# GpSimd issues the DMAs of its own weight sums, `outer` is laid out in column halves, and the hidden sums are spread one tile a group

## The chip, the cores and the metric

The program runs on one core of a Trainium2 chip. The metric is the device time of one execution in microseconds; the profile comes from one further execution of the same program. An engine's name is followed by its short form in the rows: TensorE (PE, its weight loads PEld), VectorE (DVE), ScalarE (ACT), GpSimd (POOL), SyncE (SP, which here only issues DMAs; SPq in the rows).

## The reference

4608 tokens in 8 batches of 576. First an attention within chunks of 64 tokens (8 heads of 64), then a gated layer without routing, all in float32:

```python
scores = scale * np.matmul(q_c, k_c.transpose(0, 1, 2, 4, 3))   # chunks of 64
attn = np.exp(scores - max); attn = attn / (sum + 1e-09)
x = np.matmul(attn, v_c)                                        # to [4608, 512]
gate = 1.0 / (1.0 + np.exp(-(x @ w_gate)))                      # 512 -> 1536
out = (gate * (x @ w_val)) @ w_out                              # 1536 -> 512
```

## The kernel before

**Precision.** Each float32 operand is split into a high and a low part that TensorE takes at full rate, and each product is three matmuls (high x high, low x high, high x low). The low part is always made by a subtract on VectorE after a copy on ScalarE.

**Blocks.** The tokens are nine blocks of 512. Blocks 0, 1 and 2 go through `hidden` and `down`: for each of 12 tiles `f` of the hidden width, 24 matmuls of 128x512 for gate and value, and 12 into four accumulators `acc` (one per 128 tokens); after `f` = 11 `evacuate` copies these to `ob` or, for the third and fourth of block 2, to `obs`, and stores them.

Blocks 3 to 8 go in three pairs n = 0, 1, 2. A pair uses a seven-product scheme for 2x2 block matrices, so that it has seven products where eight would stand. The *up stage* has 12 groups (6 pairs `p` of hidden tiles, gate and value), each with 7 products of 6 matmuls (`first`, `middle`, `last`); the weights of a group come from HBM as `wr` (`load_group`), half of them the blocks themselves (`given`), half of them sums of blocks (`sums`). The *down stage* has 42 *spots*, one for each of 7 products and 6 tiles `f`, with 6 matmuls each (`down_products`, L620): its weights `wd` come from `outer` (the blocks) and `outer_sums` (`load_down`), its other side are the hidden tiles and differences of them: `t1` and `t2`, made by `down_sums` on VectorE, and a further subtract of `t2` on GpSimd (L653) when the third product is reached. `down_split` makes high and low of the operand two spots ahead (six in the last pair).

**Weight sums.** `keep_sums` makes one of 36 sums on GpSimd: two adds (L359), four small ones (L363), a cast (L368) and a subtract (L369) into `a_both`, which is then stored. The first 24 are of the gate and value weights, which lie in SBUF. The last 12 are of the out weights, which have been stored to `outer` by then: they are fetched again in four DMAs into `again` (L351), a tile that has the same place as `a_both`. `keep` writes these steps into the loops: 14 sums in block 1, 16 in block 2, one each in the up groups 1 to 6 of pair 0. All the DMAs are issued by SP. The store of a sum is written one sum later, or, from the first of the 12 on, ahead of the next fetch.

**Attention of later blocks** runs beside all this: `flow` is cut into pieces, and `tick(share)` gives it credit at set places (`SHARES`), `insert` puts the matmuls of scores and values there. For a pair the flow also makes the seven operands `xc` of the next pair, once the up stage no longer uses their places; `due` issues what is left of them at once.

**What sets the order.** TensorE, VectorE and SP execute in the written order (`manual_schedule`). The order on ScalarE and GpSimd is chosen by a planner. Every engine and SP's issue is in order: an instruction that waits holds up all that follow it there. Tiles of one tag share a place, and the later one waits until all readers of the earlier are through. The places that matter: "spare" (`a_both` of every other sum, block 2's `obs`, later an `obs` of each down stage), "a_both" (the other sums, `again`, `t2`), "ob" (two buffers: `ob`, and `u3` of the up groups, written at L480).

Of the kernel before, what the change touches and what calls it, by code (L numbers as in the profile page):

```python
# [8 lines left out]
F32 = mybir.dt.float32  # L9
F32R = mybir.dt.float32r  # L10
# [5 lines left out]
P = 128  # L16
# [26 lines left out]
LAST = 2  # L43
DOWN_FROM = 0


SHARES = {1: 2.5, 2: 2.4, "up": 1.0, "down": 1.05, "turned": 0.4}


@with_exitstack  # L50
def chunk_attn_moe(ctx: ExitStack, tc: tile.TileContext, q, k, v, w, out, turned_out):
# [286 lines left out]
    def keep_outer(f):  # L338
        nc.sync.dma_start(outer[:, f], wt[f, 2].bitcast(F32))

    def keep_sums(p, which, c):

        if c == 0:
            sums[p, which] = (
                outer_sums[:, p] if which == 2 else dp.tile([P, 4, 2, 256], F32, name=f"sums{p}{which}"))
        if which == 2:
            again = sb.tile([P, 2, 2, 2, P], F32, tag="a_both", name="again")
            for n in range(2):
                src = outer[:, p + 6 * n].rearrange("p a (h c n) -> p a h c n", h=2, c=2)
                for a in range(2):  # L350
                    nc.sync.dma_start(again[:, n, a], src[:, a, :, c])  # L351
        val = sb.tile([P, 4, P], F32, name="a_val")
        for n in range(2):
            if which == 2:
                parts = again[:, n]
            else:
                parts = wt[2 * p + n, which].rearrange("p a (k c n) -> p a k c n", k=2, c=2)[:, :, :, c].bitcast(F32)
            dst = val[:, n::2] if which == 2 else val[:, 2 * n:2 * n + 2]
# [12 lines left out]

# [6 lines left out]

    groups, wo, xc, hid = {}, {}, {}, {}

    def load_group(n, p, which, parts=(0, 1)):
# [6 lines left out]
        for part in parts:  # L388
# [15 lines left out]
    def load_outer(p):  # L404
        t = place(2048)
        nc.sync.dma_start(t.bitcast(F32), outer[:, 2 * p:2 * p + 2].rearrange("p f a n -> p (f a n)"))
        t = t.rearrange("p (f a n) -> p f a n", f=2, a=2)
        wo[2 * p], wo[2 * p + 1] = t[:, 0], t[:, 1]

# [96 lines left out]

    def split(n, f, b):
        h = hid[n, f][:, b]
        hh = mp.tile([P, TB], F32R, name="hh")
        nc.scalar.copy(hh, h)  # L510
        hl = mp.tile([P, TB], F32R, name="hl")
        nc.vector.tensor_tensor(out=hl, in0=h, in1=hh.bitcast(F32), op=ALU.subtract)
        return hh, hl

    def outward(m, f, t, hh, hl):
        ts = slice(t * P, (t + 1) * P)
        if f == 0:
            acc[m, t] = ps_o.tile([P, DM], F32, tag="acc", name="acc")
        for i, (hx, wpart) in enumerate(((hh, 0), (hh, 1), (hl, 0))):
            nc.tensor.matmul(  # L520
                acc[m, t], lhsT=hx[:, ts], rhs=wo[f][:, wpart],
                start=f == 0 and i == 0, stop=f == NF - 1 and i == 2)
        if f == NF - 1:
            evacuate(m, t)


    DOWN = (1, 6, 2, 7, 5, 4, 3)
# [5 lines left out]
    def load_down(n, i):  # L533

        t = wp.tile([P, 4, 512], F32R, tag=ring["weights"][i % 4], name="wd")
        spots, k = SPOTS[4 * i:4 * i + 4], 0
        while k < len(spots):
            r, f = spots[k]
            m = len([x for x in spots[k:] if x[0] == r])
            if r in DOWN_GIVEN:  # L540
                below, h = DOWN_GIVEN[r]
                for e in range(m):
                    nc.sync.dma_start(
                        t[:, k + e].rearrange("p (a n) -> p a n", a=2).bitcast(F32),
                        outer[:, 6 * below + f + e, :, h * 256:(h + 1) * 256])
            else:
                nc.sync.dma_start(
                    t[:, k:k + m].bitcast(F32), outer_sums[:, f:f + m, DOWN_SUMS[r]].rearrange("p f c n -> p f (c n)"))
            for e in range(m):
                loaded[r, f + e] = t[:, k + e]  # L550
            k += m

    def down_lhs(r, f, wpart, c):
        x, y = (wpart, c) if r in DOWN_GIVEN else (c, wpart)
        return loaded[r, f][:, x * 256 + y * P:x * 256 + (y + 1) * P]

    def down_sums(n, p):

        if p == 0:
            t = xp.tile([P, 8, TB], F32, tag="x", name="t1")  # L560
            for f in range(8):
                t1[f] = t[:, f]
        elif p == 3:
            both = sb.tile([P, 2, TB], F32, tag="a_both", name="t2")
# [3 lines left out]
                5: mp.tile([P, TB], F32, tag="hf", bufs=1, name="t2")})  # L568
        for f in (2 * p, 2 * p + 1):
            e = f % 6  # L570
            b11, b12 = (hid[n, e][:, b] for b in range(2))
            if p < 3:
                nc.vector.tensor_tensor(out=t1[e], in0=b12, in1=b11, op=ALU.subtract)
            else:
                b22 = hid[n, f][:, 1]
                nc.vector.tensor_tensor(out=t2[e], in0=b22, in1=t1[e], op=ALU.subtract)
                nc.vector.tensor_tensor(out=b12, in0=b22, in1=b12, op=ALU.subtract)

# [29 lines left out]
    def down_products(n, between):  # L608
# [3 lines left out]
        def store(c, b, h, src):  # L612
            t = ((n - DOWN_FROM) * 2 + b) * TB
            nc.sync.dma_start(turned_out[h * 256 + c * P:h * 256 + (c + 1) * P, t:t + TB], src)
# [29 lines left out]
        for q, (r, f) in enumerate(SPOTS):  # L644
# [159 lines left out]

    made = []

    def keep(n):
        for _ in range(n):
            if kept and kept[0][1] == 2:
                while made:  # L810
                    nc.sync.dma_start(*made.pop(0))
            if kept:
                p, which, c = kept.pop(0)
                if c == 0 and which < 2:
                    keep_given(p, which)
                made.append(keep_sums(p, which, c))
            if len(made) > 1 or made and not kept:
                nc.sync.dma_start(*made.pop(0))

    for op in START.split():  # L820
        run(op)
    def rest():
# [22 lines left out]
        for n in range(3):  # L845
# [4 lines left out]
            for i, (p, which) in enumerate(order):  # L850
                if i + 1 < len(order) and i > 0:
                    load_group(n, *order[i + 1])
                if n >= DOWN_FROM and i == 8:
                    assert not kept and not made
                if i % 2 if DOWN_FROM else i:
                    keep(1)
                if pending:
# [14 lines left out]
            if n >= DOWN_FROM:  # L872
                down_begin(n)
                last(n, *order[-1])
                down_sums(n, 5)
                now["open"] = n + 1
                def between(q):
                    if n < LAST:
                        if q in (32, 36):
                            load_group(n + 1, 0, 0, ((q - 32) // 4,))  # L880
                        tick(SHARES["turned"])
                        insert(upto, 1)
                down_products(n, between)
                if n < LAST:
                    load_group(n + 1, 0, 1)
                continue
# [37 lines left out]
```

## Time and profile before

| | |
|---|---|
| median of 3 runs (lowest, highest) | 980.25 us (979.16, 980.58) |
| the profiled execution, its own time | 980.72 us |
| its span, first to last instruction | 978.9 us |
| TensorE matmul | 892.1 us busy, 91% of the span, 6004 matmuls |
| VectorE / ScalarE / GpSimd busy | 635.1 / 390.6 / 251.4 us |
| mean granted TensorE clock (1 is 2.4 GHz) | 0.963 |
| DMA | 197.63 MB, mean 202 GB/s |

The stages can be read off TensorE's instructions in order of time: blocks 0 to 2 until 357, pair 0's up stage to 549.5 and its down stage to 615.5, pair 1's to 739 and 803.7, pair 2's to 917.9 and 975.2. "Granted clock" is the mean over a stretch; TensorE runs at 1.2 or at 2.4 GHz. A matmul of 128x512 that follows another takes 0.227 us at the higher one. In the rows, what stands in brackets is the time the engine was idle before an instruction and what ended it.

### The profile page before, as it was taken

The page shows a single profiled execution, that of the slowest core. Times are in us where ns is not written, and L with a number is a line of the kernel's source. Part 1 is how long each engine was busy: PE and PEld are TensorE (multiplying, and loading weights), DVE is VectorE, ACT ScalarE, POOL GpSimd, SP SyncE. Part 2 cuts the span into 40 slices and gives each one's busy share as a digit, 9 for nine tenths or more (in the row PEclk, how much of TensorE's full clock was granted, in tenths as well). Part 3 has the DMA queues.
Part 4 walks back from the last instruction along what each step waited for, and adds up shares of the span by engine and source line. Part 5 has one row for each costly group of instructions (what it writes and reads, how often), then busy time and mean ns, then how long its engine had stood idle before and what let it go on. Part 6 is the DMA issues. An engine that isn't in the chain of part 4 may idle for free.

```text
span 978.9 us, 15513 instructions
## 1 busy us (share of the span) xinstructions
PE 892.1 (91%) x6004; PEld 725.9 (74%) x6004; DVE 635.1 (65%) x941; ACT 390.6 (40%) x716; POOL 251.4 (26%) x312
## 2 busy tenths in 40 slices
PE   4799999999999983498859899999998999999998
PEld 3678888888888862376648778888886788888886
DVE  6998963455445570365638788677768864556883
ACT  6898642333443330041304555233434531211640
POOL 0100040598888444443420030000002100000140
PEclk9899999999999997698979999999999999999999
DMA  7764222867865472577766467776546557564662
GB/s 289 248 237 151 87 71 82 286 233 241 298 233 195 138 250 86 191 250 222 236 245 212 149 206 250 264 250 215 199 132 205 185 185 268 183 214 151 215 226 97
DMA packets 119209, 197.63 MB, mean 202 GB/s; under 512 B 8544, under 2 KB 62304, under 8 KB 119136
## 3 DMA queue, kind: packets, MB, share of 16 engines
q1 hardware_dynamic: 119136, 196.64, 59.9%
q8 instruction: 48, 0.79, 0.3%
q14 instruction: 25, 0.20, 0.1%
HBM read 152.57 MB, written 44.04 MB: 201 GB/s over the span
## 4 chain that ended last, share of the span: by engine, by line
PE 67%; DMA 11%; POOL 8%; DVE 6%; ACT 3%; SPq 2%; issue 2%; POOLq 0%; DVEq 0%; ACTq 0%
PE g L273 15%; PE cy L445 12%; PE dx L620 10%; PE cz L445 8%; PE cx L445 8%; PE acc L299 7%; PE dz L620 5%; DMA outer_sums<-a_both 4%; POOL a_val L363 3%; DMA again<-outer 3%; POOL a_both L369 2%; POOL a_val L359 2%; SPq L351 2%; PE av L242 1%; PE sc L171 1%
## 5 line engine op out<-in xcount | busy, mean ns | idle before, releaser
L273 PE MATMUL g<-xt,w 128*128 128x512 f32 (+1 forms) x960 | 208.2, 372 | 5.3 <-ACT hf L282 2.2
L273 PEld LDWEIGHTS g<-xt,w 128*128 128x128 f32 x960 | 167.8, 190 | 37.4 <-ACT hf L282 2.8
L445 PE MATMUL cy<-xc,wr 128*128 128x512 f32 x648 | 164.7, 399 | 31.1 <-DVE u L480 28.9
L445 PEld LDWEIGHTS cy<-xc,wr 128*128 128x128 f32 x648 | 125.0, 194 | 60.2 <-DVE u L480 29.3
L653 POOL TENSOR_TENSOR t<-hid,t 128x512 f32<-128x512 f32 x18 | 36.6, 2055 | 408.0 <-DVE hl L596 241.8
L445 PE MATMUL cx<-xc,wr 128*128 128x512 f32 x432 | 110.6, 403 | 21.2 <-DMA wr<-given 18.7
L445 PEld LDWEIGHTS cx<-xc,wr 128*128 128x128 f32 x432 | 83.0, 194 | 40.7 <-DMA wr<-given 20.6
L445 PE MATMUL cz<-xc,wr 128*128 128x512 f32 x432 | 109.0, 396 | 0.0
L445 PEld LDWEIGHTS cz<-xc,wr 128*128 128x128 f32 x432 | 81.0, 190 | 17.3
L299 PE MATMUL acc<-w,hh 128*128 128x512 f32 x288 | 89.6, 393 | 2.4 <-ACT hh L286 2.4
L363 POOL TENSOR_TENSOR a_val<-a_val 128x128 f32<-128x128 f32 x144 | 80.4, 558 | 11.3
L620 PE MATMUL dx<-hs,wd 128*128 128x512 f32 x348 | 81.9, 390 | 0.7 <-DVE hs L596 0.7
L620 PEld LDWEIGHTS dx<-hs,wd 128*128 128x128 f32 x348 | 65.0, 188 | 14.9 <-DVE hs L596 1.5
L480 DVE TENSOR_TENSOR u<-cy,s 128x512 f32<-128x512 f32 x36 | 24.8, 689 | 72.6 <-PE cy L445 39.6
L284 DVE TENSOR_TENSOR hf<-g,hf 128x512 f32<-128x512 f32 (+1 forms) x40 | 25.5, 637 | 71.1 <-PE g L273 66.9
L463 DVE TENSOR_TENSOR u<-cy,s 128x512 f32<-128x512 f32 x36 | 24.9, 691 | 70.4 <-PE cy L445 67.1
L299 PEld LDWEIGHTS acc<-w,hh 128*128 128x128 f32 x288 | 53.3, 188 | 13.7 <-ACT hh L286 2.9
L368 POOL CAST a_both<-a_val 128x512 fp32r<-128x512 f32 x36 | 25.1, 698 | 146.4 <-DVE w_val L127 95.9
L460 ACT COPY s<-cx 128x512 f32<-128x512 f32 x36 | 21.2, 588 | 103.9 <-PE cx L445 102.3
L299 PE MATMUL acc<-w,hl 128*128 128x512 f32 x144 | 56.8, 396 | 1.3 <-DVE hl L288 1.2
L369 POOL TENSOR_TENSOR a_both<-a_val,a_both 128x512 fp32r<-128x512 f32 x36 | 48.8, 1356 | 2.9
L359 POOL TENSOR_TENSOR a_val<-w 128x256 f32<-128x256 f32 x48 | 39.7, 847 | 27.4 <-DVE w L130 25.6
(124 smaller groups left out, 1344.4 us busy)
## 6 DMA issues: line engine op xcount, KB each, us to landing
wr<-sums SPq DMA_DIRECT2D x72, 512.0 KB, 5.2
w_raw<-w_in SPq DMA_DIRECT2D x36, 512.0 KB, 5.1
wr<-given SPq DMA_DIRECT2D x36, 512.0 KB, 4.8
wd<-outer SPq DMA_DIRECT2D x54, 256.0 KB, 4.9
sums<-a_both SPq DMA_DIRECT2D x24, 512.0 KB, 5.0
wd<-outer_sums SPq DMA_DIRECT2D x12, 1024.0 KB, 5.8
qt<-q_in SPq DMA_DIRECT2D x36, 256.0 KB, 4.2
kt<-k_in SPq DMA_DIRECT2D x36, 256.0 KB, 4.3
```

Source lines behind the costliest of these rows:

```text
L273: nc.tensor.matmul(ps[:, tok], lhsT=wt[f, which][:, wpart, c:c + P], rhs=xt[m][:, part, 2 * u + i, tok], start=n == 0, stop=n == 11)
L284: nc.vector.tensor_tensor(out=hf, in0=pv, in1=hf, op=ALU.mult)
L299: nc.tensor.matmul(acc[m, t], lhsT=hx[:, ts], rhs=wt[f, 2][:, wpart], start=f == 0 and i == 0, stop=f == NF - 1 and i == 2,)
L359: nc.gpsimd.tensor_tensor(out=dst, in0=parts[:, 0], in1=parts[:, 1], op=ALU.add)
L363: nc.gpsimd.tensor_tensor(out=val[:, o], in0=val[:, x], in1=val[:, y], op=op)
L368: nc.gpsimd.tensor_copy(both[:, :, 0], val)
L369: nc.gpsimd.tensor_tensor(out=both[:, :, 1], in0=val, in1=both[:, :, 0].bitcast(F32), op=ALU.subtract)
L445: nc.tensor.matmul(bank, lhsT=lhs(wpart, c), rhs=x[:, part, c], start=start and k == 0, stop=stop and k == 5, skip_group_check=True)
L463: nc.vector.tensor_tensor(out=u2, in0=y, in1=s1, op=ALU.add)
L480: nc.vector.tensor_tensor(out=u3, in0=y, in1=s1, op=ALU.add)
L620: nc.tensor.matmul(bank[to][c], lhsT=down_lhs(r, f, wpart, c), rhs=down_in[q][part], start=r in (1, 6, 5) and (f, i) == (0, 0), stop=stop ...
L653: nc.gpsimd.tensor_tensor(out=t2[f], in0=hid[n, f + 6][:, 0], in1=t2[f], op=ALU.subtract)
```

## The change

GpSimd issues the store of each sum itself, directly behind the subtract, and the fetch of `again`: now one DMA per sum, into the place "spare", written one sum ahead, behind the two adds of the sum before. GpSimd's instructions of this part are now in the written order too. `outer` is laid out in two column halves: it is written by two DMAs per tile instead of one, and `wd` is read from it in runs of 128 elements instead of 256. In pair 0 two sums instead of one stand in an up group. `down_sums` makes one tile a group instead of two every other group, the last two at spots 2 and 4 of the down stage. The subtract of L653 goes to VectorE, one every third spot from 12 to 27. The attention's share in the down stage is 0.36 from spot 4 on instead of 0.4 from spot 0. Functions that no path used are taken out, which changes no instruction.

```diff
-SHARES = {1: 2.5, 2: 2.4, "up": 1.0, "down": 1.05, "turned": 0.4}
+SHARES = {1: 2.5, 2: 2.4, "up": 1.0, "turned": 0.36}
...
-    outer = dp.tile([P, NF, 2, DM], F32, name="outer")
+    outer = dp.tile([P, NF, 2, 4, P], F32, name="outer")
...
     def keep_outer(f):
-        nc.sync.dma_start(outer[:, f], wt[f, 2].bitcast(F32))
+        src = wt[f, 2].bitcast(F32).rearrange("p a (h c n) -> p (a h) c n", h=2, c=2)
+        for c in range(2):
+            nc.sync.dma_start(outer[:, f, c], src[:, :, c])
+
+    fetched = {}
+
+    def fetch_outer(p, c):
+
+        t = fetched[p, c] = wp.tile([P, 2, 4, P], F32, tag="spare", name="again")
+        nc.gpsimd.dma_start(t, outer[:, p::6, c])
...
-        if which == 2:
-            again = sb.tile([P, 2, 2, 2, P], F32, tag="a_both", name="again")
-            for n in range(2):
-                src = outer[:, p + 6 * n].rearrange("p a (h c n) -> p a h c n", h=2, c=2)
-                for a in range(2):
-                    nc.sync.dma_start(again[:, n, a], src[:, a, :, c])
         val = sb.tile([P, 4, P], F32, name="a_val")
         for n in range(2):
             if which == 2:
-                parts = again[:, n]
+                parts = fetched[p, c][:, n].rearrange("p (a h) n -> p a h n", a=2)
+                dst = val[:, n::2]
...
             nc.gpsimd.tensor_tensor(out=dst, in0=parts[:, 0], in1=parts[:, 1], op=ALU.add)
+        if kept and kept[0][1] == 2:
+            fetch_outer(kept[0][0], kept[0][2])
...
         nc.gpsimd.tensor_tensor(out=both[:, :, 1], in0=val, in1=both[:, :, 0].bitcast(F32), op=ALU.subtract)
-        return sums[p, which][:, :, c], both.rearrange("p s a n -> p s (a n)").bitcast(F32)
+        nc.gpsimd.dma_start(sums[p, which][:, :, c], both.rearrange("p s a n -> p s (a n)").bitcast(F32))
...
                     nc.sync.dma_start(
-                        t[:, k + e].rearrange("p (a n) -> p a n", a=2).bitcast(F32),
-                        outer[:, 6 * below + f + e, :, h * 256:(h + 1) * 256])
+                        t[:, k + e].rearrange("p (c a n) -> p c a n", c=2, a=2).bitcast(F32),
+                        outer[:, 6 * below + f + e, :, h::2])
...
             down_split(n, q + ahead_by)
-            if r == 2:
-                nc.gpsimd.tensor_tensor(out=t2[f], in0=hid[n, f + 6][:, 0], in1=t2[f], op=ALU.subtract)
+            if q in (2, 4):
+                down_sums(n, 9 + q // 2)
+            if 12 <= q < 30 and q % 3 == 0:
+                e = q // 3 - 4
+                nc.vector.tensor_tensor(out=t2[e], in0=hid[n, e + 6][:, 0], in1=t2[e], op=ALU.subtract)
...
-                made.append(keep_sums(p, which, c))
-            if len(made) > 1 or made and not kept:
-                nc.sync.dma_start(*made.pop(0))
+                keep_sums(p, which, c)
...
-                if i % 2 if DOWN_FROM else i:
-                    keep(1)
+                if i:
+                    keep(2)
...
-                    if n >= DOWN_FROM and i % 2 == 0:
-                        down_sums(n, i // 2 - 1)
+                    if i > 1:
+                        down_sums(n, i - 2)
...
-                        tick(SHARES["turned"])
+                    tick(SHARES["turned"] if q > 3 else 0)
...
-        with tc.manual_schedule(engines={mybir.EngineType.DVE, mybir.EngineType.SP}):
+        with tc.manual_schedule(engines={mybir.EngineType.DVE, mybir.EngineType.SP, mybir.EngineType.Pool}):
             rest()
```

## Rows read from the trace of the kernel before

**Rows 1.** Busy time by stage: stretch, length, busy per engine (instructions), PEclk, DMA share, GB/s.
```profile
357.00:549.50 192.50, 139.84 (x965) 109.56 (x964) 103.26 (x148) 48.46 (x87) 58.94 (x82) 0.85 0.63 206
549.50:615.50 66.00, 60.96 (x318) 49.01 (x317) 55.43 (x72) 33.56 (x56) 10.74 (x6) 0.97 0.58 192
615.50:739.00 123.50, 123.50 (x954) 101.27 (x953) 89.76 (x137) 45.53 (x77) 0.00 (x0) 1.00 0.65 218
739.00:803.70 64.70, 59.69 (x254) 47.91 (x253) 53.18 (x69) 29.84 (x48) 10.63 (x6) 0.97 0.57 186
...
917.90:975.20 57.30, 57.30 (x253) 47.11 (x251) 39.65 (x58) 20.28 (x36) 15.25 (x6) 1.00 0.56 183
```

**Rows 2.** The same view for the matmuls of scores alone (L171).
```profile
357.00:549.50 192.50, 4.65 (x256) 4.10 (x256) 0.85 0.63 206
609.00:742.00 133.00, 3.48 (x192) 3.07 (x192) 1.00 0.65 218
```

**Rows 3.** The same view for the matmuls of values alone (L242).
```profile
357.00:549.50 192.50, 3.48 (x192) 3.07 (x192) 0.85 0.63 206
609.00:742.00 133.00, 4.64 (x256) 4.10 (x256) 1.00 0.65 218
```

**Rows 4.** Chain that ended last, a stretch of block 0: start, us, what.
```profile
68.73 2.72 PE acc L299 x12
```

**Rows 5.** Waits of PE, 280 to 620 us: total us, times, longest.
```profile
PE cy L445 <- DVE u L480: 28.9, 1, 28.9
PE cx L445 <- DMA wr<-given: 18.7, 3, 11.6
...
PE cx L445 <- ACT obs L315: 2.4, 1, 2.4
```

**Rows 6.** Waits of the whole span.
```profile
DVE u L480 <- DMA out<-ob: 32.8, 1, 32.8
```

**Rows 7.** SP's issues in order of time: start, length, line, transfer.
```profile
398.82 2.09 SPq L351 DMA_DIRECT2D again<-outer  x4
400.96 0.93 SPq L318 DMA_DIRECT2D out<-ob  x2
```

**Rows 8.** GpSimd in order of time, one add of a sum of out weights.
```profile
389.82 0.72 POOL L359 TENSOR_TENSOR a_val<-again 128x256 f32<-128x256 f32 x1 [6.16 <-DMA again<-outer]
```

**Rows 9.** GpSimd's groups, whole span: count, busy us, mean ns, idle before.
```profile
L363 POOL TENSOR_TENSOR a_val<-a_val 128x128 f32<-128x128 f32 x144 | 80.4, 558 | 11.3
L369 POOL TENSOR_TENSOR a_both<-a_val,a_both 128x512 fp32r<-128x512 f32 x36 | 48.8, 1356 | 2.9
L359 POOL TENSOR_TENSOR a_val<-w 128x256 f32<-128x256 f32 x48 | 39.7, 847 | 27.4 <-DVE w L130 25.6
L653 POOL TENSOR_TENSOR t<-hid,t 128x512 f32<-128x512 f32 x18 | 36.6, 2055 | 408.0 <-DVE hl L596 241.8 <-DVE hs L596 165.5 <-POOL t L653 0.7
L368 POOL CAST a_both<-a_val 128x512 fp32r<-128x512 f32 x36 | 25.1, 698 | 146.4 <-DVE w_val L127 95.9 <-DMA sums<-a_both 48.8
```

**Rows 10.** GpSimd in order of time, the cast of the third sum.
```profile
178.68 0.70 POOL L368 CAST a_both<-a_val 128x512 fp32r<-128x512 f32 x1 [37.07 <-DMA sums<-a_both]
```

**Rows 11.** ScalarE in order of time, the end of block 2.
```profile
363.87 0.58 ACT L315 COPY obs<-acc 128x512 f32<-128x512 f32 x1
```

**Rows 12.** SP's issues of the sums' stores: ns shortest, median, longest.
```profile
L818 SPq DMA_DIRECT2D sums<-a_both x23: 513/661/1129, 174.2 to 324.4; - x23
```

**Rows 13.** DMA issues, whole span: count, size of each, median us to landing.
```profile
wr<-sums SPq DMA_DIRECT2D x72, 512.0 KB, 5.2
wd<-outer SPq DMA_DIRECT2D x54, 256.0 KB, 4.9
sums<-a_both SPq DMA_DIRECT2D x24, 512.0 KB, 5.0
```

**Rows 14.** PE in order of time, third spot of pair 1's down stage.
```profile
744.66 0.80 PE L620 MATMUL dx<-hl,wd 128*128 128x512 f32 x1 [2.61 <-DVE hl L596]
```

**Rows 15.** VectorE in order of time, same stage.
```profile
741.50 0.69 DVE L576 TENSOR_TENSOR t<-hid,t 128x512 f32<-128x512 f32 x1
...
754.72 2.33 DVE L435 TENSOR_TENSOR xc<-raw,xc 128x1024 fp32r<-128x1024 f32 x1
```

More of the change, by code (lines that the diff above doesn't have):

```diff
@@ L354, in keep_sums @@
             if which == 2:
-                parts = again[:, n]
+                parts = fetched[p, c][:, n].rearrange("p (a h) n -> p a h n", a=2)
+                dst = val[:, n::2]
             else:
                 parts = wt[2 * p + n, which].rearrange("p a (k c n) -> p a k c n", k=2, c=2)[:, :, :, c].bitcast(F32)
-            dst = val[:, n::2] if which == 2 else val[:, 2 * n:2 * n + 2]
+                dst = val[:, 2 * n:2 * n + 2]
             nc.gpsimd.tensor_tensor(out=dst, in0=parts[:, 0], in1=parts[:, 1], op=ALU.add)
+        if kept and kept[0][1] == 2:
+            fetch_outer(kept[0][0], kept[0][2])
         for o, x, y, op in ((3, 2, 3, ALU.add), (2, 0, 2, ALU.subtract), (0, 3, 0, ALU.subtract), (1, 1, 0, ALU.subtract)):
@@ L377, in place @@
         return wp.tile([P, n], F32R, tag=rotation[-1], name="wr")
-    groups, wo, xc, hid = {}, {}, {}, {}
+    groups, xc, hid = {}, {}, {}
     def load_group(n, p, which, parts=(0, 1)):
@@ L402, in load_group @@
                 lhs.update({4: (of_given(t, 0), "T4"), 3: (of_sums(t, 1), "B22"), 7: (of_sums(t, 2), "T3")})
[L404 to L408, printed above, removed]
     MADE = (
@@ L505, in last @@
             gated(n, f, 1, u2)
[L507 to L524, printed above, removed]
     DOWN = (1, 6, 2, 7, 5, 4, 3)
@@ L553, in down_lhs, with down_sums @@
     def down_lhs(r, f, wpart, c):
[L554 to L559, printed above, removed]
+        return loaded[r, f][:, (2 * c + wpart) * P:(2 * c + wpart + 1) * P]
+    def down_sums(n, f):
+        if f == 0:
             t = xp.tile([P, 8, TB], F32, tag="x", name="t1")
-            for f in range(8):
-                t1[f] = t[:, f]
-        elif p == 3:
+            for e in range(8):
+                t1[e] = t[:, e]
+        elif f == 6:
             both = sb.tile([P, 2, TB], F32, tag="a_both", name="t2")
@@ L568, in down_sums @@
                 5: mp.tile([P, TB], F32, tag="hf", bufs=1, name="t2")})
[L569 to L577, printed above, removed]
+        e = f % 6
+        b11, b12 = (hid[n, e][:, b] for b in range(2))
+        if f < 6:
+            nc.vector.tensor_tensor(out=t1[e], in0=b12, in1=b11, op=ALU.subtract)
+        else:
+            b22 = hid[n, f][:, 1]
+            nc.vector.tensor_tensor(out=t2[e], in0=b22, in1=t1[e], op=ALU.subtract)
+            nc.vector.tensor_tensor(out=b12, in0=b22, in1=b12, op=ALU.subtract)
     FREED = (0, 5, 2, 4, 1, 6, 3)
@@ L803, in chunk_attn_moe @@
     kept += [(f, 2, c) for f in range(6) for c in range(2)]
-    made = []
     def keep(n):
         for _ in range(n):
-            if kept and kept[0][1] == 2:
-                while made:
-                    nc.sync.dma_start(*made.pop(0))
             if kept:
@@ L852, in rest @@
                     load_group(n, *order[i + 1])
-                if n >= DOWN_FROM and i == 8:
-                    assert not kept and not made
-                if i % 2 if DOWN_FROM else i:
-                    keep(1)
+                if i:
+                    keep(2)
                 if pending:
@@ L871, in rest, with between @@
                 insert(upto, 1)
[L872 to L880, printed above, removed]
-                        tick(SHARES["turned"])
-                        insert(upto, 1)
-                down_products(n, between)
-                if n < LAST:
-                    load_group(n + 1, 0, 1)
-                continue
+            down_begin(n)
+            last(n, *order[-1])
+            now["open"] = n + 1
+            def between(q):
+                if n < LAST:
+                    if q in (32, 36):
+                        load_group(n + 1, 0, 0, ((q - 32) // 4,))
+                    tick(SHARES["turned"] if q > 3 else 0)
+                    insert(upto, 1)
+            down_products(n, between)
+            if n < LAST:
+                load_group(n + 1, 0, 1)
     with tc.manual_schedule(engines={mybir.EngineType.PE}):
@@ L916 @@
     args[-1] = args[-1].bitcast(U32)
-    rows = (FIRST_PAIR + 2 * DOWN_FROM) * TB
+    rows = FIRST_PAIR * TB
     out = nc.dram_tensor("out", (rows, DM), F32, kind="ExternalOutput").ap()
```

4 lines of the change are left out of this document (1 added, 3 removed).

## The prediction

> **What bounds the kernel now.** I read the busy time by stage first, then who waited for whom, then the queues of SP and GpSimd in order of time. TensorE is the engine to watch: in the second pair's up stage it is busy 123.50 of 123.5 us, in the third pair's down stage 57.30 of 57.3 [rows 1]. So a stage whose feeding works takes exactly its matmuls, and the losses stand in three places. The first pair's up stage takes 192.5 us with 139.84 busy, at a granted clock of 0.85. The down stages of pairs 0 and 1 take 66.0 and 64.7 us where the third takes 57.3 [rows 1].
>
> The up stages of pairs 0 and 1 do the same work: 504 matmuls of products, and seven attention inserts, four of scores and three of values in the first, three and four in the second (64 small matmuls each) [rows 2, 3]. Pair 0 carries 12 matmuls of block 2 more, 2.7 us at full clock [rows 4]. So it loses 192.5 - 123.5 - 2.7 = 66.3 us. The waits name it: 28.9 us on a VectorE add, 18.7 us on loads of weights, 2.4 us on the copy of an accumulator [rows 5]; the rest of the 66 is mostly matmuls at the 1.2 GHz level after these pauses (0.85 granted).
>
> Why was the VectorE add late? It waited 32.8 us for the store `out<-ob` [rows 6], whose buffer it writes. That store was issued at 400.96, right behind the loads `again` at 398.82 [rows 7]. SP issues in written order, and in this stretch the order holds 12 rounds of: load `again`, wait for GpSimd's sum, store it, wait for the store to land, because `again` takes its buffer. GpSimd for its part waits 6.16 us for `again` in such a round [rows 8]. Everything else on SP, stores of `out` and loads of `wr`, stands behind this ring of about 12 us a round. Both late groups of [rows 5] are that one cause.
>
> **The change part by part.**
>
> *SP is freed.* The 36 stores and the 48 loads `again` (now 12 larger ones) leave SP's queue, so nothing on SP waits for GpSimd until the first down stage loads its sums. `out<-ob` then goes out when its copy is done, and `wr` loads go when a place is free, as in pair 1. Of the 66.3 us I let 6 stay: the 2.4 us for the accumulator's copy is untouched, two or three waits under 1 us beside it stay, and the slow matmuls behind them are worth some 2. Gain 60.3 us.
>
> *GpSimd's own line, the new critical one.* Its work per sum is two adds, four small ones, a cast and a subtract: 2 x 0.847 + 4 x 0.558 + 0.698 + 1.356 = 5.98 us [rows 9], with eight gaps of 0.07 about 6.5. Call d the time that one DMA issue holds GpSimd; no row of this trace shows one. At 178.68 - 37.07 = 141.6 it stood ready for the third cast and waited 37 us for a store on SP [rows 10]; that wait goes. From there: cast and subtract of the third sum 2.1, then 21 sums x 6.5 = 137, so 281 + 24 d for the first 24 with their stores. The first `again` is fetched one sum ahead (one d), and six sums of the out weights are written before block 2's end, each with a store and a fetch: 39 + 12 d. The adds of the 31st take 1.8 more: 322 + 37 d. Who waits for that? The tile `again` now lives in the place "spare", and so does `obs`, into which ScalarE copies block 2's fourth accumulator at 363.9 [rows 11]; the fetch for the 31st sum is written before it. Behind that copy stand ScalarE's and VectorE's next copies, and TensorE for the PSUM banks. So there is a new wait of 322 + 37 d - 363.9 us, and it costs nothing up to d = 1.13.
>
> Bounds for d: below, the 0.51 us that SP takes for the issue of the very same store at its shortest [rows 12]; above, 5.0 us, if GpSimd were held until the store has landed [rows 13]. I take 0.5 to 1.1, by the nearest row (the same transfer, another queue; its median is 0.66), so no wait. The fetch has 4.5 us + d to land, against 5.2 for a load of its size [rows 13], so a microsecond a sum may be lost there as well; the six of them eat the margin that d leaves, hardly more.
>
> No row prices an issue on GpSimd; the Trainium skill does ("DMA: Bandwidth & Descriptors", section "Latency and other measured facts": about 1 us to the first byte on the software path against 0.6 on the hardware one). By that, as an estimate from that page, the 31st adds end at 359, just before the copy, and the sum below stands.
>
> After the 31st, six sums of 6.5 + 2 d remain, done near 420, and the first down stage begins near 489: covered, unless d is above 5.
>
> *SP's additions.* 24 stores of `outer` halves instead of 12, in a stretch where TensorE waits for nothing on SP: nothing. In the down stages the `wd<-outer` loads read runs of half the length; all but a stage's first two are issued eight spots, 8 x 6 matmuls, 10.9 us at the rate of [rows 4], before their use and land in 4.9 [rows 13]; the first two go out ahead of the last group's products, with less to spare, and no matmul waits for them today: nothing, as long as landing does not double.
>
> *Down stages.* Pair 0 has one values insert (4.64 x 64 / 256 = 1.2 us [rows 3]), so the excess over 57.3 is 7.5 and 7.4 us. Two causes show. First, TensorE waits 2.61 us for `hl` at the stage's third spot [rows 14], because four VectorE subtracts, the first at 741.50, 0.69 each, stand ahead of it [rows 15]. They move to spots 2 and 4, behind that split, and no attention credit is given before spot 4. Second, VectorE slows beside GpSimd's six `t2` subtracts: an `xc` subtract takes 2.33 us [rows 15] while one of those runs, 2.06 us each in the mean against 1.36 for the same shape elsewhere [rows 9]. They move to VectorE: 6 x 0.69 = 4.1 us per stage. VectorE has 53.18 us in pair 1's stage [rows 1]; plus 4.1 less what it no longer loses beside GpSimd (six overlaps of about 0.7, so some 4) it stays near 53 of 59. So a wait of a microsecond or two stays at the spots where an add, an operand and a split fall together. The smaller attention share (38 x 0.36 = 13.7 credits instead of 42 x 0.4 = 16.8; the operands need 13.2) pushes the last operands to the stage's end, at worst one subtract of 1.2 us late. I let 2.5 us stay in each: gain 5.0 and 4.9, about 10. From below, VectorE at 57 with no relief leaves no gain or a loss of 2 each; from above, the whole 7.5. In pair 2 VectorE is not the limit and GpSimd's subtracts cost TensorE nothing: zero. The single subtracts spread over the up stages fill VectorE's free time there (89.76 of 123.5 busy [rows 1]): zero.
>
> **The sum.** The profiled execution took 980.72 us (span 978.9), half a microsecond over the median of 980.25. 980.7 - 60.3 - 10 = 910.4: I say 910. Its own range is 900 (everything goes: 66.3 + 14.9) to 921 (the down stages give nothing).
>
> **The rivals.**
>
> *GpSimd is late.* d between 1.13 and 3. The new wait is 37 d - 42: with d = 2 some 32 us, 943; the case spans 912 to 980. For it: 512 runs per store have to be described by the engine that also adds, and the threshold is near. Against it: the same store takes SP 0.66.
>
> *The DMA engines are crowded.* From 357 on the last six sums put 6.3 MB into about 50 us, 126 GB/s, beside a stage that draws 218 at a share of 0.65 [rows 1]; 0.65 scales to 335 at full share, and 344 are wanted. If the `wr` loads waited for all of these bytes: 6.3 MB at 335 GB/s = 19 us, 929. Against it: only the first half of one stage, and a place holds a load two groups ahead.
>
> *Slower than before: GpSimd's issue takes over 3 us.* Same place, same wait on "spare", other size: the 70 us gained are eaten at 37 d - 42 = 70, d = 3.0. With d at 5.0 the wait is 143 us: 1053. It would come from GpSimd being held until its transfers move, or shut out by VectorE as the `t2` subtracts were [rows 9]. Against it: those lost 0.7 each, not 2.
>
> A rule of the Trainium skill would produce just that ("SBUF — State Buffer", section "SBUF: two separate sides"): while VectorE runs an instruction that takes both ports, GpSimd can't write descriptors; a transfer of 0.62 us became 3.1 there. By that price, as an estimate, the wait would be 73 us and the time 983. VectorE's work beside these sums is nearly all two-input subtracts and reductions, which that page does not count among the two-port instructions, so I hold it unlikely.
>
> *It does not free the queue.* SP, in written order, may have a further wait in that stretch (it waits for TensorE at scores, values and places) that keeps the stores late; 970 to 981. Against it: the same waits stand in pair 1's order, and TensorE lost nothing there.
>
> **How the numbers follow.** Forecast 0.56, GpSimd late 0.25, crowded 0.08, issue over 3 us 0.07, queue not freed 0.04. From 900 to 945 lie the forecast, the crowd and two thirds of the late case (d up to 2, the likelier part of it): four fifths. What differs by less than 0.2%, 2 us, is no change for a measurement of this kernel. Faster: 0.56 + 0.25 + 0.08 + half of the last, 0.91; within 0.2%: 0.02; slower 0.07.
>
> **What would show it.** Right: the first pair's up stage takes about 132 us at a clock near 1; no wait of VectorE for `out<-ob`; GpSimd's casts from 142 on without the 37 us; the 31st adds before 364; the down stages of pairs 0 and 1 near 60, with no wait for `hl` at the third spot. Wrong: ScalarE's copy into `obs` waiting for GpSimd or starting after 370 with TensorE idle there (late); `wr` landing over 10 us with TensorE waiting (crowded); VectorE without gaps and TensorE waiting for it in the middle of the down stages (the 10 us not won).

## The result and the profile after

The changed kernel takes 908.2 us (906.68 to 908.7), beside 980.41 us (979.16 to 982.27) for the kernel before on the same chip: a ratio of 0.926, interval 0.9241 to 0.9278. Forecast were 910 us, 900 to 945. The profiled execution took 908.14 us (span 906.4, mean granted clock 0.989 instead of 0.963), 72.6 less than the 980.72 from which the sum was made.

The busy time by stage of the changed kernel, columns and stages as in [rows 1] (core time, length, PE, PEld, DVE, ACT, POOL busy, PEclk, DMA share, GB/s):

```profile
356.80:490.30 133.50, 128.83 (x966) 104.11 (x965) 105.86 (x149) 49.40 (x88) 42.41 (x57) 0.99 0.76 258
490.30:549.80 59.50, 59.27 (x317) 47.94 (x316) 51.54 (x76) 33.15 (x52) 0.00 (x0) 1.00 0.69 213
549.80:673.30 123.50, 123.50 (x954) 101.31 (x953) 91.77 (x138) 46.06 (x81) 0.00 (x0) 1.00 0.65 218
673.30:731.10 57.80, 57.72 (x254) 47.19 (x253) 51.22 (x75) 30.17 (x48) 0.00 (x0) 1.00 0.67 209
...
845.30:902.60 57.30, 57.29 (x253) 47.15 (x251) 39.01 (x64) 20.33 (x36) 0.00 (x0) 1.00 0.60 184
```

Against [rows 1] the first pair's up stage lost 59 us (192.5 to 133.5), its clock went from 0.85 to 0.99, and the down stages of pairs 0 and 1 lost 6.5 and 6.9. The second pair's up stage and the third's down stage, where nothing was to be had, stand at 123.5 and 57.3 as before. So 72.4 of the 72.6 us came from the three places that the forecast named.

Who waited for whom in pair 0's up stage (356.8 to 490.3 us), the same view as [rows 5]: of 50 us in three groups 2.5 are left, and beside them stand two small waits.

```profile
PE cx L444 <- ACT obs L314: 2.5, 1, 2.5
PE acc L298 <- ACT hh L285: 1.4, 1, 1.4
PE cy L444 <- DVE u L462: 0.9, 1, 0.9
```

GpSimd in order of time, in brackets the idle time before and what ended it:

```profile
141.00 0.61 POOL L373 CAST a_both<-a_val 128x512 fp32r<-128x512 f32 x1
143.38 0.73 POOL L375 DMA_DIRECT2D sums<-a_both  x1 [0.40 <-POOL a_both L374]
...
353.60 1.44 POOL L362 TENSOR_TENSOR a_val<-again 128x256 f32<-128x256 f32 x2
371.97 0.73 POOL L347 DMA_DIRECT2D again<-outer  x1 [16.93 <-DVE sums L697]
...
427.84 0.77 POOL L375 DMA_DIRECT2D outer_sums<-a_both  x1 [0.46 <-POOL a_both L374]
```

The third cast starts at 141.00 where it started at 178.68 after a wait of 37.07 [rows 10]. An issue shows up as an instruction of 0.73 us, 0.40 us after the subtract that it stores: GpSimd's issue waits for the end of its own instruction before. The 31st sum's adds end at 353.60 + 1.44 = 355.04. Then GpSimd waits 16.93 us before the fetch into "spare". (The releaser shown, a reduction on VectorE, has nothing to do with that place. What the fetch has to wait for are the stores of block 2's `obs`, next below: in the run with halves the profile names `out<-obs` for this fetch, and with the copies in "ob" the wait is gone.)

SP and ScalarE at the same place, against [rows 7] and [rows 11]: the copy into `obs` runs at 364.81, 9.8 us after those adds, and `out<-ob` goes out at 366.79, where it stood at 400.96.

```profile
364.81 0.58 ACT L314 COPY obs<-acc 128x512 f32<-128x512 f32 x1
```
```profile
366.79 0.82 SPq L317 DMA_DIRECT2D out<-ob  x2
367.70 0.89 SPq L317 DMA_DIRECT2D out<-obs  x2
```

GpSimd's groups of the changed kernel (count, busy us, mean ns, idle before): what no row of before could price.

```profile
L375 POOL DMA_DIRECT2D sums<-a_both x24 | 17.7, 736 | 9.6 <-POOL a_both L374 9.6
L375 POOL DMA_DIRECT2D outer_sums<-a_both x12 | 9.3, 776 | 4.9 <-POOL a_both L374 4.9
```

### The profile page after: what moved, and what is told of

The parts are those of the page before. It is cut to its first block, busy times and chain, and to the rows that moved or that the text cites. A ratio compares the mean times of both kernels' runs of the same rounds, so it can differ in the third digit from the quotient of the medians.

```text
span 906.4 us, 15445 instructions
## 1 busy us (share of the span) xinstructions
PE 877.4 (97%) x6004; PEld 718.5 (79%) x6004; DVE 638.2 (70%) x959; ACT 390.3 (43%) x716; POOL 245.6 (27%) x342
## 3 DMA queue, kind: packets, MB, share of 16 engines
q1 hardware_dynamic: 111840, 171.47, 57.8%
## 4 chain that ended last, share of the span: by engine, by line
PE 88%; DVE 6%; ACT 2%; DMA 2%; issue 1%; SPq 0%; DVEq 0%; ACTq 0%
PE g L272 20%; PE cy L444 16%; PE dx L597 12%; PE cz L444 11%; PE cx L444 11%; PE acc L298 9%; PE dz L597 5%; PE av L241 2%; PE sc L170 2%; DVE w_raw L124 1%; DMA w_raw<-w_in 1%; DVE w L129 0%; DMA vt<-v_in 0%; DMA kt<-k_in 0%; DVE w_raw L126 0%
## 5 line engine op out<-in xcount | busy, mean ns | idle before, releaser
L444 PE MATMUL cy<-xc,wr 128*128 128x512 f32 x648 | 160.4, 392 | 0.9 <-DVE u L462 0.9
L444 PEld LDWEIGHTS cy<-xc,wr 128*128 128x128 f32 x648 | 122.5, 189 | 27.1 <-DVE u L462 1.6
L444 PE MATMUL cx<-xc,wr 128*128 128x512 f32 x432 | 104.9, 391 | 2.5 <-ACT obs L314 2.5
L444 PEld LDWEIGHTS cx<-xc,wr 128*128 128x128 f32 x432 | 81.0, 188 | 19.6 <-ACT obs L314 2.9
L368 POOL TENSOR_TENSOR a_val<-a_val 128x128 f32<-128x128 f32 x144 | 77.9, 541 | 10.6
L287 DVE TENSOR_TENSOR hl<-hf,hh 128x512 fp32r<-128x512 f32 (+1 forms) x40 | 31.5, 787 | 21.4 <-ACT hh L285 21.3
```

Source lines behind the costliest of these rows:

```text
L287: nc.vector.tensor_tensor(out=hl[:, tok], in0=hf, in1=hh[:, tok].bitcast(F32), op=ALU.subtract)
L444: nc.tensor.matmul(bank, lhsT=lhs(wpart, c), rhs=x[:, part, c], start=start and k == 0, stop=stop and k == 5, skip_group_check=True)
```

## The experiments

The theory: the gain of the up stage comes from GpSimd issuing its own DMAs, because the queue in which a store waits is then the one that makes it ready; its price is GpSimd's time, and it shows only past the moment when `obs` needs the place "spare". The down stages gain by two edits, each for one wait. The rivals: the new places and the earlier fetch would have done without GpSimd as issuer; GpSimd's issue time is irrelevant; one of the two down edits gives everything.

**SP issues, all else as changed.**

```diff
-        nc.gpsimd.dma_start(t, outer[:, p::6, c])
+        nc.sync.dma_start(t, outer[:, p::6, c])
...
-        nc.gpsimd.dma_start(sums[p, which][:, :, c], both.rearrange("p s a n -> p s (a n)").bitcast(F32))
+        nc.sync.dma_start(sums[p, which][:, :, c], both.rearrange("p s a n -> p s (a n)").bitcast(F32))
```

> The changed kernel with SP as the issuer of the 36 stores and 12 fetches again; places, one-sum-ahead fetch, order, layout and everything in the down stages stay as changed. My theory: what cost the time was SP standing in order behind GpSimd's sums, in a ring that also had a load and a store's landing in it. The ring is now shorter (no landing of the store, the fetch is ahead), so SP is held only by GpSimd's own 6.5 us a sum. At block 2's end SP is nearly level with it, so out<-ob goes out in time; but in the up groups 1 to 3 of pair 0 two sums, 13 us of GpSimd, stand in a group of 10 us, and the wr loads of three groups stand behind them: 5 to 15 us late, 913 to 925. Rival A, the issuing engine does not matter and only the places and the fetch ahead do: 908, within 1%. Rival B, being in SP's queue is all that matters: up stage of pair 0 near 190 us again, 965.

Measured: 941.31 us (939.97 to 942.14), ratio 0.960 (0.9575 to 0.9619). Missed: it is 33 us slower than the changed kernel, where at most 17 were expected, and it lies between the two rivals (908 and 965). TensorE's waits of this kernel are those of before on a smaller scale:

```profile
PE cy L444 <- DVE u L462: 15.4, 1, 15.4
PE cx L444 <- DMA wr<-given: 12.6, 3, 5.9
```

SP's issues in order of time show why, and GpSimd's adds behind the fetch of 356.00:

```profile
346.72 0.44 SPq L399 DMA_DIRECT2D wr<-sums  x1
354.16 0.32 SPq L396 DMA_DIRECT2D wr<-given  x1
...
356.00 0.53 SPq L347 DMA_DIRECT2D again<-outer  x1
356.63 0.55 SPq L375 DMA_DIRECT2D outer_sums<-a_both  x1
365.10 0.53 SPq L347 DMA_DIRECT2D again<-outer  x1
...
380.52 0.36 SPq L375 DMA_DIRECT2D outer_sums<-a_both  x1
380.93 1.48 SPq L317 DMA_DIRECT2D out<-ob  x2
```
```profile
362.55 2.52 POOL L362 TENSOR_TENSOR a_val<-again 128x256 f32<-128x256 f32 x2 [13.86 <-DMA again<-outer]
```

The expectation took SP to be level with GpSimd at block 2's end. It was not: from 346.72 to 354.16 SP stands before a `wr` load, whose place TensorE still reads, and the fetch of `again` stands behind it. GpSimd then waits 13.86 us for that fetch, and the four sums of which SP has still to issue fetches and stores push `out<-ob` to 380.93. The queue couples both ways: TensorE holds up GpSimd through SP, and GpSimd then TensorE. Of the 57.5 us that the whole up part is worth (980.4 - 908.2 = 72.2, less 14.7 of the down stages by the run below), 33.1 come from the issuer, with all else as changed; 24.4 come from the rest: fetch ahead, one DMA instead of four, other places, GpSimd's written order, two sums a group.

**Each store in two DMAs**, which doubles GpSimd's issues of stores:

```diff
-        nc.gpsimd.dma_start(sums[p, which][:, :, c], both...)
+        for s in range(0, 4, 2):
+            nc.gpsimd.dma_start(sums[p, which][:, s:s + 2, c], both[:, s:s + 2]...)
```

> Each sum's store is issued by GpSimd as two DMAs of 256 KB (tiles 0 and 1, tiles 2 and 3) instead of one. My theory: GpSimd's line up to the 31st sum's adds is the new critical one behind the place 'spare'. A second issue costs 0.74 us more (its profile shows 0.74 per issue, and 0.41 of wait before the first only); 30 stores stand before the 31st adds, so these end at 355 + 22 = 377 instead of 355, and the copies into obs, at 364.8 in the changed kernel, wait for them: 12 us later, TensorE idle behind them and some 2 us of slow clock: 920 to 924. Rival: the line has more slack than that, or another wait sets the start of pair 0: 908, no change.

Measured: 926.3 us (925.93 to 927.27), ratio 0.945 (0.9426 to 0.9468), 2 us over the expected 920 to 924, and by the expected wait. All engines at the end of block 2, in order of time:

```profile
380.79 1.41 POOL L362 TENSOR_TENSOR a_val<-again 128x256 f32<-128x256 f32 x2
382.23 0.59 ACT L314 COPY obs<-acc 128x512 f32<-128x512 f32 x1 [15.33 <-POOL a_val L362]
382.87 2.93 PE L446 MATMUL cx<-xc,wr 128*128 128x512 f32 x6 [19.18 <-ACT obs L314]
```

The 31st adds end at 382.20, and 0.03 us later the copy into `obs` starts, then TensorE. The copy is 17.4 us later than in the changed kernel, the time 18.1.

**The same two DMAs, but the two `obs` copies go to places of the tag "ob"**:

```diff
-        if m < FIRST_PAIR - 1 or t < 2:
-            ob = mp.tile([P, DM], F32, name="ob")
-        else:
...
+        ob = mp.tile([P, DM], F32, name="ob")
```

> As the kernel with stores in halves, but block 2's third and fourth output tiles go through the place 'ob' as those of blocks 0 and 1 do, so nothing that TensorE waits for shares a place with 'again'. My theory: the 12 to 16 us of the kernel with halves go, although GpSimd is as late; the third and fourth copy now wait for the stores of the first two to land, some 3 us: 908 to 913, and GpSimd's 17 us wait before the 32nd fetch is gone too. Rival: the halves cost by their DMA count or by holding GpSimd from its later sums, not by the place: 920 to 924 as before.

Measured: 910.17 us (909.05 to 910.69), ratio 0.928 (0.9255 to 0.9305). As expected: GpSimd's line is just as late (the 31st adds end at 381.41, against 382.20 with halves alone), and it costs 2 us instead of 18.

```profile
380.00 1.41 POOL L357 TENSOR_TENSOR a_val<-again 128x256 f32<-128x256 f32 x2
```

The place "spare" was the link that cost the time. Some 2 us stay; they are not traced, but TensorE's wait for ScalarE's copy is 3.7 us there and 2.5 in the changed kernel.

**The store in four DMAs**, with "spare" and then through "ob" (`range(0, 4, 1)` and `s:s + 1` in the edits above):

> Each of the 36 stores goes out in four DMAs on GpSimd instead of one. With halves the 31st sum's adds ended at 382.2 us, 27 later than with whole stores, and the time rose by 18. If every added issue holds GpSimd for 0.73 us plus a gap of 0.07, the 60 more issues ahead of the 31st adds put their end at 382.2 + 60 x 0.80 = 430, ScalarE's copy into obs waits 62 to 66 us, and the time is 908.2 + 65 = 973 (966 to 980), near the kernel before. Rival (an issue costs by its size, so that quarters cost half of a half's issue): 382.2 + 24 + some 5, a time of 930 to 945.

Measured: 944.38 us (943.88 to 945.94), ratio 0.964 (0.9617 to 0.966). Missed, 29 us under the forecast. The rival's range held it, but its price did not hold either: a quarter costs three quarters of a half's issue, not half. The rows of the engines in order of time:

```profile
129.79 2.29 POOL L376 DMA_DIRECT2D sums<-a_both  x4 [0.32 <-POOL a_both L374]
...
399.34 1.41 POOL L362 TENSOR_TENSOR a_val<-again 128x256 f32<-128x256 f32 x2
...
400.78 0.58 ACT L314 COPY obs<-acc 128x512 f32<-128x512 f32 x1 [34.93 <-POOL a_val L362]
401.42 2.93 PE L446 MATMUL cx<-xc,wr 128*128 128x512 f32 x6 [38.02 <-ACT obs L314]
```

A quarter's issue takes 547 ns in the mean, not 732 as a half's: four take 2.17 us where two halves take 1.45. So a sum grew by 0.72 instead of 1.6 us, and 30 sums by 21.6; the adds came 18.6 later than with halves (the first cast, 1.8 us earlier, takes off part; the rest, some 1 us, is not traced). The mechanism held where the price did not: the copy into `obs` is 36.0 us later than in the changed kernel (400.78 against 364.81), the time is 36.2 longer. Three kernels now lie on one line, a microsecond of that copy for a microsecond of time.

> The same four DMAs a store, with block 2's last two accumulators copied into places of the name ob, so that none of them waits for the place spare. What is left is the first down stage: with whole stores GpSimd's last store ended at 428, and 36 x 3 x 0.80 = 86 us more put it at some 514, 24 us after that stage begins at 490 (the prediction held this covered up to an issue time of 5; by the last store of the changed kernel the cover is 62 us, used up by 78 more issues). The stage takes the sums over its whole length, so part of it is still covered: 912 to 930, with TensorE waiting on loads of sums in pair 0's down stage and nowhere else. Rival (the spare place is not all that the line holds up): 940 to 975, with waits already in the up stage of pair 0.

Measured: 909.21 us (908.08 to 910.25), ratio 0.9275 (0.9257 to 0.9294), 3 us under the expected range, and without the wait expected in the down stage. At the cheaper issue the last store is issued by 466, and in the changed kernel that stage begins at 490:

```profile
464.07 2.17 POOL L371 DMA_DIRECT2D outer_sums<-a_both  x4 [0.41 <-POOL a_both L369]
```

**The down-stage part undone** (`down_sums` in twos, its last two at the stage's start, the `t2` subtracts on GpSimd, share 0.4 from the first spot):

```diff
-            if q in (2, 4):
-                down_sums(n, 9 + q // 2)
-            if 12 <= q < 30 and q % 3 == 0:
...
+            if r == 2:
+                nc.gpsimd.tensor_tensor(out=t2[f], in0=hid[n, f + 6][:, 0], in1=t2[f], op=ALU.subtract)
...
+            down_sums(n, 10), down_sums(n, 11)
...
-                    tick(SHARES["turned"] if q > 3 else 0)
+                    tick(SHARES["turned"])
```

> The changed kernel with the down-stage part undone: t2's subtract on GpSimd at the third product, down_sums two tiles every other group and the last two tiles ahead of the down stage, attention share 0.4 from spot 0. My theory: the two parts are independent, the down stages of pairs 0 and 1 go back from 59.5 and 57.8 us to 66 and 64.7: 13.4 us, 921 to 923. Rival: the down part is worth less when GpSimd no longer stands in SP's queue, or more since VectorE's work in the up stage is denser now: 912 or 930.

Measured: 922.9 us (921.77 to 923.25), ratio 0.941 (0.9388 to 0.9429). As expected: the down part is worth 14.7 us, the up part 57.5. TensorE in order of time, and the granted clock around the pause (length, PE busy, PEclk, DMA share, GB/s), from that kernel:

```profile
495.35 0.50 PE L597 MATMUL dx<-hl,wd 128*128 128x512 f32 x1 [2.61 <-DVE hl L573]
511.16 0.63 PE L597 MATMUL dx<-hl,wd 128*128 128x512 f32 x1 [1.81 <-DVE hl L573]
```
```profile
500.00:510.00 10.00, 9.34 (x41) 1.00 1.05 325
510.00:520.00 10.00, 8.84 (x32) 0.83 0.44 146
```

The second wait is followed by a stretch at 0.83: part of it ran at the lower of the two clock levels. That is the part of the cost that no wait shows.

**One of the two down edits at a time.** The `t2` subtracts back on GpSimd (the `r == 2` lines above alone):

> The changed kernel with t2's second subtract back on GpSimd at the third product; the rest of the down-stage part stays. My theory: the two parts of the down stages' loss are separate. This one is VectorE slowed beside GpSimd (an xc subtract of 2.33 us instead of 1.22): the waits behind it in the kernel before, 1.52 and 0.90 us in pair 0, 1.52 and 0.74 in pair 1, come back with their slow matmuls, about 3 us a stage: 913 to 915. Rival: it was the share of the attention and the early subtracts that made room, and GpSimd's help would now be free: 908, or faster, since VectorE has 4 us less to do per stage.

Measured: 916.56 us (912.67 to 917.87), ratio 0.9325 (0.9302 to 0.9347), 8.4 over the changed kernel and 1.6 over the expected 913 to 915. Its runs scatter the most of all, and by the profile the two down stages lose 6.7 (61.6 and 62.4 against 59.5 and 57.8), where some 6 were expected. Its longest pause of TensorE in order of time, VectorE's split that ends it, the clock behind it (length, PE busy, PEclk, DMA share, GB/s), and GpSimd's group of subtracts, 1928 ns each:

```profile
697.12 0.50 PE L597 MATMUL dx<-hl,wd 128*128 128x512 f32 x1 [2.25 <-DVE hl L573]
```
```profile
695.31 1.75 DVE L573 TENSOR_TENSOR hl<-t,hh 128x512 fp32r<-128x512 f32 x1
```
```profile
697.12:700.00 2.88, 2.88 (x8) 0.61 0.00 0
```
```profile
L632 POOL TENSOR_TENSOR t<-hid,t 128x512 f32<-128x512 f32 x12 | 22.9, 1928 | 244.2 <-DVE hl L573 243.6 <-DVE hs L573 0.6
```

That split takes 0.69 us in the changed kernel (686 ns in the mean); here five of GpSimd's subtracts run from 685.25 to 696.52.

The last two `down_sums` tiles ahead of the stage instead of at spots 2 and 4 (the `q in (2, 4)` and `down_sums(n, 10)` lines above alone):

> The changed kernel with the last two tiles of down_sums ahead of the down stage instead of at spots 2 and 4. My theory: the wait for hl at the third spot comes back, 2.6 us in pairs 0 and 1, with 1 to 2 us of slow matmuls: 915 to 917. Pair 2 splits six spots ahead and doesn't notice. Rival: the wait at the third spot went because the attention gets no credit before spot 4, not because of the four subtracts: 908 to 910.

Measured: 916.91 us (916.03 to 917.78), ratio 0.934 (0.9324 to 0.936). As expected; 8.1 us in the two stages. The old wait of [rows 14] is back in both, and the clock falls behind it:

```profile
497.10 0.79 PE L597 MATMUL dx<-hl,wd 128*128 128x512 f32 x1 [2.62 <-DVE hl L573]
684.08 0.50 PE L597 MATMUL dx<-hl,wd 128*128 128x512 f32 x1 [2.61 <-DVE hl L573]
```
```profile
497.10:500.00 2.90, 2.90 (x7) 0.50 0.22 55
...
684.08:687.00 2.92, 2.92 (x8) 0.58 0.15 43
```

So a wait of 2.6 us in a stage is worth some 4 in time: 2.9 us at about half the clock are some 1.4 us more. Neither edit alone gives the 14.7; by the stages the two losses add up to 14.8 (6.7 and 8.1).

**The share 0.4 from the first spot** (`SHARES["turned"]` and its `tick` alone):

> The changed kernel with the attention's share in the down stages back at 0.4 from spot 0. My theory: small; one 1.2 us subtract may fall between the splits of the first spots where the tiles of down_sums now stand too, a wait of a microsecond a stage, and operands come a little earlier: 908 to 911. Rival: the share is what cured the start of the stage: 913 to 916.

Measured: 909.59 us (909.24 to 911.36), ratio 0.927 (0.9253 to 0.9289). As expected, and no difference that this can tell (1.4 us, the intervals overlap): no gain is shown for the credit.

**The turn from block 2 to pair 0**, the last place with waits (2.5 + 1.4 + 0.9 us): block 2 takes one insert piece at a time, and none of its attention work falls on its last tile.

```diff
-                tick(SHARES[m])
-                insert(upto, 2)
+                share, pieces = SHARES[m] if (m, f) != (2, 11) else 0, 2 if m == 1 else 1
+                tick(share)
+                insert(upto, pieces)
```

> The changed kernel with block 2's attention inserted one tick earlier (pieces 1 instead of 2) and no attention credit in its last tile, so that the operand subtracts of pair 0 end before block 2's last copies instead of standing ahead of them. The up stage of pair 0 still loses 133.4 - 123.5 - 2.7 = 7.2 us, all at its first products: waits of 1.36, 2.45 and 0.85 us and slow matmuls behind them. My theory: VectorE's and ScalarE's operand work ahead of the copies is their cause, so 3 to 6 us go: 902 to 905, as long as the 31st sum's adds (355) still end before the copies, now near 361. Rival: the waits are the plain chain of copy and add at the change from block 2 to pair 0, which no order shortens: 908.

Measured: 904.84 us (902.06 to 906.42), ratio 0.922 (0.9193 to 0.9238), as expected. Since the gain is near the measurement's own width, it ran once more beside the changed kernel on one chip:

> The changed kernel once more, as a yardstick for the next one on the same chip: 906.5 to 909.

> The transition version once more (block 2 takes one insert piece a spot and none in its last-but-one position's ticks). If its gain of some 3 us is real, it is 903 to 905.5 and 2 to 4 us below the changed kernel on the same chip, and no wait of cx for obs stands in the trace. Rival (spread between chips only): within 1 us of the changed kernel.

Measured: 907.36 us (906.26 to 909.82) and 904.5 us (903.13 to 905.8); ratios 0.926 (0.9238 to 0.9282) and 0.9227 (0.9209 to 0.9246), both as expected. A gain of 2.9 here and 3.4 before: the same sign and size twice, though the intervals of this pair just overlap. TensorE of the faster kernel (its second run), where the changed one waits 2.45 us for `obs`:

```profile
363.69 1.65 PE L444 MATMUL cx<-xc,wr 128*128 128x512 f32 x6 [0.59 <-DVE ob L316]
```

## Why the prediction was right

*SP freed: 60.3 us forecast, 59.0 measured* (the stage is 133.5 us where 132.2 were forecast). The prediction left 6 us in the stage, and 7.3 are there: 2.5 for the copy, where it had 2.4, two more waits (0.9, and 1.4 where it had them under 1), and some 2.5 of slow matmuls, where it had 2. The rule behind it, that an instruction which waits holds all behind it, is what the run with SP as issuer shows, in both directions. What the prediction did not separate is how much of the term belongs to the issuer: 33 of 57.5 us.

Here a rule of the Trainium skill would have misled ("DMA: Bandwidth & Descriptors", section "Issuing engines are not separate DMA queues"): issuing from several engines only saves the sequencer's time for the issues. In the stage where the run with SP as issuer lost its time (30.4 us of TensorE's waits), SP issues nine stores and eight fetches, of 0.37 and 0.53 us by their medians: 7.6 us of the sequencer, against 33 that the change of the issuer gave. The 31 issues before that stage cost TensorE nothing: it begins at 356.7 there and at 356.8 in the changed kernel. What it saved is waiting in order, not issuing.

*GpSimd's line: 322 + 37 d, no wait up to d = 1.13.* No wait came, and the line is right in kind; but d is at the upper edge of 0.5 to 1.1, not near the 0.66 of the row that the prediction leaned on. The issue itself takes 0.73 to 0.78 us, and some 0.40 stand before it. By the distances between GpSimd's instructions, less the gap of 0.07 that the prediction counted anyway, an issue adds 1.02 us in the first 24 sums, 1.09 for a fetch and 1.14 in the later sums: 1.05 in the mean, close to the prediction's second estimate of 1. So the line gives 322 + 37 x 1.05 = 361, and the adds ended at 355.0. Most of the rest is that a sum took less work: 6.1 us where little disturbs it (casts at 155.01 and 162.09, 7.08 apart, less 1.02) and 6.3 in the mean of the 27 in question, where 6.5 were counted, which is 5 us. The margin of 9.8 us before the copy is what decided; doubling the issues used it up and cost 18 us. So the rival "GpSimd is late" was near in the sense that mattered: one more issue a sum away. Its place, its mechanism and its size (every microsecond past 364.8 goes into the time) were those of the experiment. What the line lacked is the wait of 16.93 us behind the 31st adds: the last store was issued by 428.6 and not near 420, which cost nothing, since the first down stage begins at 490.

*Down stages: 10 us forecast, 13.4 measured* (6.5 + 6.9 by the stages, 14.7 by undoing them). This term was mis-sized, by 3.4 us, and together with the 1.3 us too much of the first it makes the distance from 910 to 908: that it is so short is partly luck, two errors of opposite sign. The prediction let 2.5 us stay in each stage; 1.0 stays in the first and 0.5 in the second, and no wait of TensorE is left in either. What it undercounted is what VectorE gets back when GpSimd's subtracts no longer run beside it. VectorE's groups in pair 0's down stage, of the kernel before and then of the changed one:

```profile
L596 DVE TENSOR_TENSOR hl<-t,hh 128x512 fp32r<-128x512 f32 x10 | 8.9, 903 | 3.4 <-ACT hh L595 3.4
...
L424 DVE TENSOR_TENSOR raw<-raw 128x1024 f32<-128x1024 f32 x4 | 6.0, 1490 | 0.0
```
```profile
L573 DVE TENSOR_TENSOR hl<-t,hh 128x512 fp32r<-128x512 f32 x10 | 6.6, 688 | 0.0
...
L423 DVE TENSOR_TENSOR raw<-raw 128x1024 f32<-128x1024 f32 x4 | 4.9, 1219 | 0.0
L633 DVE TENSOR_TENSOR t<-hid,t 128x512 f32<-128x512 f32 x6 | 4.1, 686 | 0.0
```

VectorE took on the 4.1 us of subtracts and yet is busy 51.54 us where it was 55.43 [rows 1]. In pair 1's stage, where the forecast had it stay near 53, it went from 53.18 to 51.22: 6.1 us came back, where some 4 were counted. That this is why no wait of a microsecond or two stayed is argued; what the run with the subtracts back on GpSimd shows is that slower splits bring such waits.

*The rivals.* Crowded DMA: the up stage draws 258 GB/s at a share of 0.76, `wr<-sums` lands in 5.4 us (5.2 before, [rows 13]), and no wait for `wr` is left. Issue over 3 us: none of the 48 issues does; the longest takes 0.84 us. The starvation rule quoted in the prediction was not seen, as the prediction thought likely for VectorE's work here. Queue not freed: `out<-ob` goes out within 0.1 us of VectorE's copy that ends at 366.77.

What stays open: how the 24.4 us which the new places and the earlier fetch give with SP as issuer divide among the places, the earlier fetch, the one DMA in place of four, GpSimd's written order and the two sums a group; no run separates these.

## What to carry to other kernels

When a queue that serves several engines holds an instruction that waits for a slow one, look at what stands behind it, and let the engine that makes the data issue the transfer; what is saved are the waits in order, which can be far more than the issue times. Price the move on the engine that takes it over, as a line up to the first moment when someone else needs a place that it holds: within that margin it is free, past it each microsecond is one of time. And look for what a pause costs after it ends: a wait of 2.6 us of TensorE was worth about 4, since the clock fell for a while.

## What was not expected of the hardware

A DMA issue on GpSimd takes 0.73 to 0.78 us in the mean for a store of 512 KB or of 256 KB, and 0.55 us for one of 128 KB, so it does not halve with the size; in each case the first of them starts 0.3 to 0.46 us after the end of the instruction that made the data.

GpSimd and VectorE are both slower in one stretch where each subtracts. In the changed kernel a GpSimd subtract takes 2.15 us beside VectorE's subtracts of 128x1024, and 1.30 without them; two of those take 4.97 us in that stretch and 2.46 later:

```profile
350.24 2.15 POOL L374 TENSOR_TENSOR a_both<-a_val,a_both 128x512 fp32r<-128x512 f32 x1
...
376.44 1.30 POOL L374 TENSOR_TENSOR a_both<-a_val,a_both 128x512 fp32r<-128x512 f32 x1
```
```profile
351.16 4.97 DVE L434 TENSOR_TENSOR xc<-raw,xc 128x1024 fp32r<-128x1024 f32 x2
...
363.70 2.46 DVE L434 TENSOR_TENSOR xc<-raw,xc 128x1024 fp32r<-128x1024 f32 x2
```

The issues are not slowed with them: 0.78 us at 352.80, in the same stretch.
